# Moving the output banks and three early chunks into the projections' PSUM banks, with a fifth first-layer weight buffer

## The chip, the cores and the metric

The kernel runs on one NeuronCore of a Trainium2 chip, as one program. The metric is the device time of one execution in microseconds (us), as the median of several runs. The engines are TensorE (PE, with its weight loads as PEld), VectorE (DVE), ScalarE (ACT), GpSimd (POOL) and SyncE (SP), which here only issues DMAs. They run side by side, each through its own instructions in a fixed order, and wait for each other by semaphores.

## What is computed

Three layers in a row, all in fp32: random-feature attention, a network with `h - tanh(h)` between two matrices, and a mixture of four networks with `relu`, weighted by token. Cut to what matters:

```python
def phi(x):                                  # x: (2, 8, 576, 64), omega: (128, 64)
    proj = einsum('bhsd,md->bhsm', x, omega)
    h = proj - sum(x * x) / 2
    return exp(h - max(h)) / sqrt(128)
q_p, k_p = phi(q * scale), phi(k * scale)
num = q_p @ (k_p.T @ v)                      # per batch and head
x = num / (q_p @ sum(k_p) + 1e-6)            # -> (1152, 512)
h = x @ w_in                                 # 512 -> 2048, first network
x = (h - tanh(h)) @ w_out                    # 2048 -> 512
p = probs / sum(probs)
out = sum_e p[:, e] * (relu(x @ w1[e]) @ w2[e])   # 4 networks, 512 -> 1024 -> 512
```

## The kernel before

**Matrices in two parts.** Every operand of a large product is split (`split`, L70) into a high part (ACT) and the rest (DVE, or POOL where `nc.gpsimd` is given), and each product is three matmuls: high·high, high·low, low·high. The weights of the first network arrive as 64-bit numbers and are put together by `Decoded` (L94): ACT `scaled` and `topped` or DVE `joined`, then `parted`, in which ACT makes the high part (`wah`, `wbh`) and POOL the low one (`wal`, `wbl`). They lie in the pool `wp` with `NJ` = 4 buffers of each name. `load_a(i, j)` is tile j (128 hidden units) of unit i (512 hidden units) of `w_in`; `ready` (L163) does all steps of a tile at once.

**Attention.** Tokens are taken in groups; the queries in 12 units (4 pairs of heads × 3 chunks of tokens, L389), and the loop at L485 works on four units at once, each a step further: transpose (`psT`) and project (`psP`, two banks of `ps_p`), turn the features (`psQ`), multiply (`psN`), transpose back (`psX`) and split into `xT`, the four pairs of tiles `x0p`, `x1p` of the first network's input (in rows `x`).

**Early chunks.** The first network's first unit (i = 0) does not wait for all tokens. `early(e)` (L471) takes tile j = e mod 4 and token chunk n = e div 4, with 512, 384 and 256 columns for n = 0, 1, 2: twelve matmuls (`hidden`, L426, rows at L435) into one bank, `pse`, of the pool `ps_e` (2 banks), then `minus_tanh` (L441) on it: ACT `u`, `t`, `q` and `m`, DVE `a`, `b`, `s` and `c`, ACT `h` and POOL `l`. In rows they are u L445, y L446, t L447, u L448 on ACT, y L449, y L450, pse L451, y L452 on DVE, hh L453 on ACT and hl L454 on POOL. L452, the copy-predicated, is the last to read the bank. e0 to e7 are started in the loop at L485, e8 to e11 behind it (L498), and after e8, e9 and e10 one tile of unit 1 (`load_a` (1,0), (1,1), (1,2)) is made ready; it takes the weight buffers of the tile that this chunk read last.

**First network.** After `actx.close()` (L502) the eight PSUM banks are given out anew: `ps_o` (2 banks, output chunks `po`), `ps_hb` and `ps_ha` (3 each, `psh`, the hidden tiles of unit 1 and later). `ps_o` comes first and lies where `ps_e` lay. `out_a` (L526) makes one output chunk of 384 columns in twelve matmuls (rows at L539); the loop at L705 puts out chunks and hidden tiles in turn. The first output chunk reads columns 0 to 383 of unit 0, the third columns 768 to 1151. A pool that opens with `reuse_waits="tile"` makes each new tile wait for the last users of just the banks or bytes it covers.

**Second network.** From about 290 us on; it reads `w1` through `wa` tiles of `wp` as well, on every other step from a pool of its own (`high`, L601).

**Order.** Up to the loop at L705 a scheduler sets the order on each engine, from the program's order and the tiles; it may move a step ahead of others. From L701 on, and again from L799, the order on DVE, PE and ACT is written out by hand. DMAs stand in program order on SP's queue.

Of the kernel before, what the change touches and what calls it, by code (L numbers as in the profile page):

```python
# [8 lines left out]
F32 = mybir.dt.float32  # L9
F32R = mybir.dt.float32r  # L10
# [16 lines left out]
def tile_favor_attention__then__two_moe(  # L27
# [19 lines left out]
    B, H, S, D = q.shape  # L47
# [4 lines left out]
    P = 128  # L52
    NP = H // 2
# [3 lines left out]
    UF = 512  # L57
    NJ = UF // P
# [7 lines left out]
    wp = ctx.enter_context(tc.tile_pool(name="wp", bufs=NJ))  # L66
# [3 lines left out]
    def split(hi, lo, src, eng_lo=None):  # L70
        nc.scalar.activation(hi, src, AF.Copy)  # L71
        (eng_lo or nc.vector).tensor_tensor(out=lo, in0=src, in1=hi.bitcast(F32), op=ALU.subtract)  # L72

    def run(todo):
        for step in todo:
            step()
# [14 lines left out]
    PLAIN = 2  # L91
    wa, wb, late = {}, {}, {}

    class Decoded:  # L94


# [26 lines left out]
            nc.vector.scalar_tensor_tensor(out=m, in0=self.up, scalar=SIGN, in1=m, op0=ALU.bitwise_and, op1=ALU.bitwise_or)  # L123

        def parted(self):
            hi = wp.tile([P, UF], F32R, tag=self.tag + "h", name=self.tag + "h")
            lo = wp.tile([P, UF], F32R, tag=self.tag + "l", name=self.tag + "l")
            split(hi, lo, self.m.bitcast(F32), nc.gpsimd)
            return hi, lo

    class Loaded:
# [10 lines left out]
        joined = scaled  # L142

        def parted(self):
            hi = self.pool.tile([P, UF], F32R, tag=self.tag + "h", name=self.tag + "h")
            lo = self.pool.tile([P, UF], F32R, tag=self.tag + "l", name=self.tag + "l")
            split(hi, lo, self.raw)
            return hi, lo

# [13 lines left out]
    def ready(load, table, *ij):  # L163
        w = load(*ij)
        w.scaled()
        w.joined()
        table[ij] = w.parted()
# [11 lines left out]
    actx = ExitStack()  # L179
    ps_e = actx.enter_context(tc.tile_pool(name="ps_e", bufs=2, space=bass.MemoryType.PSUM))  # L180
    ac = actx.enter_context(tc.tile_pool(name="ac", bufs=1))
    a2 = actx.enter_context(tc.tile_pool(name="a2", bufs=2))
    a3 = actx.enter_context(tc.tile_pool(name="a3", bufs=3))
    ps_t = actx.enter_context(tc.tile_pool(name="ps_t", bufs=2, space=bass.MemoryType.PSUM))
    ps_p = actx.enter_context(tc.tile_pool(name="ps_p", bufs=2, space=bass.MemoryType.PSUM))
    ps_n = actx.enter_context(tc.tile_pool(name="ps_n", bufs=2, space=bass.MemoryType.PSUM))
    kctx = ExitStack()
    kp = kctx.enter_context(tc.tile_pool(name="kp", bufs=2, side="right"))
    TD = TB * D
# [10 lines left out]

        nc.sync.dma_start(out=to, in_=x[b, :, REST, :].rearrange("h r d -> r h d"))

    om = ac.tile([P, 2, D], F32, name="om")
    nc.sync.dma_start(out=om, in_=omega.rearrange("m (o d) -> m o d", o=1).to_broadcast([M, 2, D]))

    def load_k(p):
# [40 lines left out]

    pso = ps_t.tile([P, 512], F32, tag="t", name="pso")
    nc.tensor.transpose(pso[:, :P], om.rearrange("p j d -> p (j d)"), ident)
    oms = ac.tile([P, P], F32, name="oms")  # L250
    nc.scalar.mul(oms, pso[:, :P], scale)
    ob = [ac.tile([P, 2 * P], F32R, name=f"ob{a}") for a in range(2)]
    for a in range(2):
# [138 lines left out]
    def q_emit(u, what, i):  # L392
        if 0 <= u < len(q_units):
            if u not in q_steps:
                p, n = q_units[u]
                qf = a3.tile([P, TB, 2, M], F32, tag="xf", name="qf")
                rest = qr[:, 2 * p:2 * p + 2, :].rearrange("p h d -> p (h d)")
                T, R = features(lambda b, h: qn[:, b, 2 * p + h], rest, chunks[n], qf, a2)
                A, Z, X = q_products(p, chunks[n], qf)
                q_steps[u] = dict(T=T, R=R, A=A, Z=Z, X=X)  # L400
            if i < len(q_steps[u][what]):
                q_steps[u][what][i]()
# [19 lines left out]
    def new_g(i, j):  # L422
        pool = late["hpb"] if i % 2 or i >= NA else hpa
        gs[i, j] = tuple(pool.tile([P, N], F32R, tag="h" + z, name="h" + z) for z in "hl")

    def hidden(i, j, chunks=range(NC), bank=None, kks=range(KD)):  # L426
        if bank is None and chunks[0] == 0 and kks[0] == 0:
            ph[i, j] = late["ps_hb" if j % 2 else "ps_ha"].tile([P, NC, 512], F32, tag="h", name="psh")
        wh, wl = wa[i, j]
        for kk in kks:  # L430
            c = slice(kk * P, (kk + 1) * P)
            xh, xl = state["x"][kk]
            for z, (w, x) in enumerate(((wh, xh), (wh, xl), (wl, xh))):
                for n in chunks:
                    nc.tensor.matmul(  # L435
                        ph[i, j][:, n, :CH] if bank is None else bank, w[:, c],
                        x[:, n * CH:(n + 1) * CH] if bank is None else x[:, n],
                        start=z == 0 and kk == 0, stop=z == 2 and kk == KD - 1,
                    )
# [31 lines left out]
    def early(e):  # L471

        j, n = e % NJ, e // NJ
        if n == 0:
            new_g(0, j)
        s = slice(chunks[n][0][0] * P, (chunks[n][-1][0] + chunks[n][-1][1]) * P)
        w = s.stop - s.start
        ps = ps_e.tile([P, 512], F32, tag="e", name="pse")[:, :w]
        hidden(0, j, [s], ps)
        t, u, y = (a2.tile([P, 512], F32, tag=z, name=z)[:, :w] for z in "tuy")  # L480
        g = minus_tanh(ps, gs[0, j][0][:, s], gs[0, j][1][:, s], t, u, y, lambda z: z, nc.gpsimd)
        run(g[x] for x in "utqambsch" + "l")

    NU = len(q_units)
    for u in range(1, NU + 3):  # L485
        q_emit(u, "R", 0)
        q_emit(u - 1, "A", 0)
        q_emit(u - 2, "Z", 0)
        q_emit(u + 1, "T", 0)
        q_emit(u, "R", 1)  # L490
        q_emit(u - 1, "A", 1)
        q_emit(u - 2, "Z", 1)
        q_emit(u - 3, "X", 0)
        if u >= NP + 3:
            early(u - NP - 3)
        if u in LATER:
            ready(*LATER[u])
    for e in range(NU - NP, NU):  # L498
        early(e)
        if e < NU - 1:  # L500
            ready(load_a, wa, 1, e % NJ)
    actx.close()  # L502


# [13 lines left out]
    late["gp"] = moe1.enter_context(tc.tile_pool(name="gp", bufs=1, side="right", reuse_waits="tile"))  # L518
    late["hpb"] = ctx.enter_context(tc.tile_pool(name="hpb", bufs=NJ, reuse_waits="tile"))
    accp = ctx.enter_context(tc.tile_pool(name="accp", bufs=1, reuse_waits="tile"))  # L520
    ps_o = ctx.enter_context(tc.tile_pool(name="ps_o", bufs=2, space=bass.MemoryType.PSUM, reuse_waits="tile"))
    plain = ExitStack()
    for z in ("ps_hb", "ps_ha"):
        late[z] = plain.enter_context(tc.tile_pool(name=z, bufs=1, space=bass.MemoryType.PSUM, reuse_waits="tile"))
# [47 lines left out]
    class Sums:  # L572
# [28 lines left out]
        def high(self, i):  # L601
            src, names = self._dest(i)
            pool = wp if self.q % 2 else late["wp"]
            w = [pool.tile([P, UF], F32R, tag="wa" + z, name="wa" + z) for z in "hl"]
            w = [x.rearrange("p (s k n) -> p s k n", s=2, n=P) for x in w]
            for s, name in enumerate(names):
                self.lhs[name] = (w[0][:, s], w[1][:, s])
            if i == 0:
                w = [x.rearrange("p s k n -> p (s k) n") for x in w]
            elif i == 3:  # L610
                w = [x[:, 0] for x in w]
            self.w = src, w[0], w[1]
            nc.scalar.activation(w[0], src, AF.Copy)
# [295 lines left out]
```

## Time and profile before

| | us |
|---|---|
| median of 3 runs | 692.48 (691.49 to 692.78) |
| profiled execution, its own time | 694.46 |
| its span | 692.6 |
| PE busy in the span | 671.7 (97%) |
| DVE busy | 530.7 (77%) |
| ACT busy | 318.0 (46%) |
| POOL busy | 61.3 (9%) |

Times in the profile count from the start of the span. PE is the engine that is nearly always busy, so the time is its work and its few gaps. A row of a timeline gives start, duration, engine, line, operation, output<-input by the program's names, shape and count; in square brackets stand the engine's idle time just before and the instruction that ended it. Matmuls overlap: a row's duration is longer than the step from one start to the next.

### The profile page before, as it was taken

Reading aid. Unit: us, or ns where it says so; the run is one execution under the profiler, and the core shown is the slowest. Engines: PE = TensorE matmul, PEld = TensorE weight load, DVE = VectorE, ACT = ScalarE, POOL = GpSimd, SP = SyncE. Lnnn points to the kernel's source line nnn. Section 1 sums busy time; section 2 is a strip of 40 time slices with the busy share of each in tenths; the row PEclk is TensorE's granted clock in tenths of the full one; section 3 lists DMA queues with packets and bytes.
Section 4 is the critical chain, followed back from the end, with each engine's and each line's share of the span. In section 5 each row is a group of like instructions: output and inputs, shape, how many; then the busy total and the mean of one; then the engine's idle time right before and its main releaser. Section 6 shows DMA issues by size and latency. Waiting matters only on the chain.

```text
span 692.6 us, 10155 instructions
## 1 busy us (share of the span) xinstructions
PE 671.7 (97%) x4059; PEld 624.7 (90%) x4059; DVE 530.7 (77%) x824; ACT 318.0 (46%) x591; POOL 61.3 (9%) x58
## 2 busy tenths in 40 slices
PE   6999998899999999899999999999999999999997
PEld 5899987899999999799999899999998999999996
DVE  4599888589999987769467687777777777777664
ACT  5699898576775754435123222322222322223120
POOL 1032023412321210000000000000000000000000
PEclk9999999999999999999999999999999999999999
DMA  8953110022221222101110112111210211120004
GB/s 223 280 164 115 62 32 1 31 76 79 92 91 62 92 62 91 31 1 62 30 31 31 55 38 62 31 40 53 61 31 31 62 49 44 31 62 1 1 0 137
DMA packets 42766, 43.72 MB, mean 63 GB/s; under 512 B 5600, under 2 KB 37600, under 8 KB 42720
## 3 DMA queue, kind: packets, MB, share of 16 engines
q1 hardware_dynamic: 42720, 43.08, 20.5%
q8 instruction: 32, 0.52, 0.3%
q14 instruction: 14, 0.11, 0.1%
HBM read 40.72 MB, written 2.36 MB: 62 GB/s over the span
## 4 chain that ended last, share of the span: by engine, by line
PE 75%; DVE 13%; ACT 6%; issue 2%; DMA 1%; SPq 1%; POOL 0%; DVEq 0%; POOLq 0%
PE po L660 28%; PE Y L643 22%; PE psh L435 7%; PE po L539 6%; PE pse L435 3%; PE psP L294 2%; PE psN L346 2%; DVE y L449 2%; DVE y L452 2%; DVE y L450 1%; ACT y L446 1%; DVE psh L451 1%; ACT u L445 1%; DVE m L123 1%; DVE m L122 1%
## 5 line engine op out<-in xcount | busy, mean ns | idle before, releaser
L666 DVE SCALAR_TENSOR_TENSOR oacc<-po,pr,oacc 128x512 f32<-128x512 f32 (+1 forms) x136 | 101.4, 746 | 34.2 <-PE po L660 33.8
L660 PE MATMUL po<-wbh,hl 128*128 128x512 f32 x290 | 112.9, 389 | 0.4 <-DVE hl L466 0.4
L660 PE MATMUL po<-wbh,hh 128*128 128x512 f32 x290 | 112.9, 389 | 0.1
L660 PE MATMUL po<-wbl,hh 128*128 128x512 f32 x290 | 112.9, 389 | 0.0
L660 PEld LDWEIGHTS po<-wbh,hl 128*128 128x128 f32 x290 | 54.4, 188 | 12.3 <-DVE hl L466 0.8
L539 PE MATMUL po<-hh,wbh 128*128 128x384 f32 x180 | 61.4, 341 | 2.1 <-DVE y L452 1.8
L660 PEld LDWEIGHTS po<-wbh,hh 128*128 128x128 f32 x290 | 54.7, 188 | 8.2 <-DVE oacc L666 0.3
L539 PE MATMUL po<-hh,wbl 128*128 128x384 f32 x180 | 61.1, 339 | 0.5 <-POOL wbl L72 0.5
L539 PE MATMUL po<-hl,wbh 128*128 128x384 f32 x180 | 61.3, 340 | 0.2 <-DVE hl L454 0.2
L660 PEld LDWEIGHTS po<-wbl,hh 128*128 128x128 f32 x290 | 54.4, 188 | 7.5
L821 ACT ACTIVATE hh<-Y 128x576 fp32r<-128x576 f32 x42 | 27.4, 653 | 72.5 <-DVE Y L818 64.0
L435 PE MATMUL psh<-x,wah 128*128 128x384 f32 x288 | 58.4, 338 | 0.6 <-ACT wah L71 0.6
L643 PE MATMUL Y<-y,wah 128*128 128x288 f32 x336 | 57.9, 294 | 0.0
L643 PEld LDWEIGHTS Y<-y,wah 128*128 128x128 f32 x336 | 51.2, 188 | 3.6 <-DVE hl L466 0.3
L435 PEld LDWEIGHTS psh<-x,wah 128*128 128x128 f32 x288 | 51.1, 190 | 0.8 <-ACT wah L71 0.8
L643 PE MATMUL Y<-Th,wal 128*128 128x288 f32 x224 | 47.8, 295 | 0.0
L643 PE MATMUL Y<-Tl,wah 128*128 128x288 f32 x224 | 47.6, 294 | 0.0
L643 PE MATMUL Y<-Th,wah 128*128 128x288 f32 x224 | 47.6, 293 | 0.0
L821 ACT ACTIVATE hh<-u 128x576 fp32r<-128x576 f32 x14 | 9.6, 688 | 73.5 <-DVE u L818 73.5
L643 PEld LDWEIGHTS Y<-Th,wah 128*128 128x128 f32 x224 | 39.0, 188 | 4.5
L453 ACT ACTIVATE hh<-y 128x1152 fp32r<-128x1152 f32 (+3 forms) x24 | 20.4, 848 | 43.1 <-DVE y L452 43.1
L539 PEld LDWEIGHTS po<-hh,wbh 128*128 128x128 f32 x180 | 34.2, 190 | 2.9 <-DVE y L452 2.0
(138 smaller groups left out, 1459.3 us busy)
## 6 DMA issues: line engine op xcount, KB each, us to landing
raw<-in_moe_w_dram SPq DMA_DIRECT2D x30, 512.0 KB, 3.5
raw<-in_moe_w_in_dram SPq DMA_DIRECT2D x16, 512.0 KB, 3.6
raw<-in_moe_w_out_dram SPq DMA_DIRECT2D x16, 512.0 KB, 3.4
kn<-in_k_dram SPq DMA_DIRECT2D x8, 256.0 KB, 4.7
vs<-in_v_dram SPq DMA_DIRECT2D x8, 256.0 KB, 4.6
qn<-in_q_dram SPq DMA_DIRECT2D x8, 256.0 KB, 4.8
out_dram<-oacc SPq DMA_DIRECT2D x7, 256.0 KB, 2.3
raw<-in_moe_w_dram SPq DMA_DIRECT2D x4, 256.0 KB, 3.6
```

The lines of the kernel that those rows point to most:

```text
L122: nc.vector.scalar_tensor_tensor(out=m, in0=self.y.bitcast(I32), scalar=3, in1=m, op0=ALU.logical_shift_left, op1=ALU.bitwise_or)
L294: nc.tensor.matmul(ps[:, i].rearrange("p a m -> p (a m)"), x[:, c], o, start=j == 0, stop=j == 2)
L346: nc.tensor.matmul(ps[:, j, h, :ZC], qt[g][:, j, h, :], kvz[p][:, t // (TB + 1), h, :], start=True, stop=True)
L435: nc.tensor.matmul(ph[i, j][:, n, :CH] if bank is None else bank, w[:, c], x[:, n * CH:(n + 1) * CH] if bank is None else x[:, n], start=z ...
L449: a=lambda: vec.scalar_tensor_tensor(out=y, in0=y, scalar=CB, in1=u, op0=ALU.add, op1=ALU.mult),
L452: c=lambda: vec.copy_predicated(view(y), view(u).bitcast(I32), ps),
L453: h=lambda: act.activation(hh, y, AF.Copy),
L539: nc.tensor.matmul(po[:, :CH], w[:, r], g[:, s], start=j == 0 and z == 0, stop=j == NJ - 1 and z == 2,)
L643: nc.tensor.matmul(ps[:, m, :HN // 2], w[:, kk], b[:, m * HN // 2:(m + 1) * HN // 2], start=first and kk == 0 and z == 0, stop=kk == 1 and ...
L660: nc.tensor.matmul(po, g[:, s], w[:, cols], start=j == 0 and z == 0, stop=j == 1 and z == 2)
L666: nc.vector.scalar_tensor_tensor(out=acc, in0=po, scalar=pr[:, t, e:e + 1], in1=acc, op0=ALU.mult, op1=ALU.add)
L821: nc.scalar.activation(halves(gs[NA + q, f][0][:, h * HN:(h + 1) * HN]), x, AF.Relu)
```

## The change

Four edits. The pools `ps_n` and `ps_p` swap places, and `ps_o` opens from the right side, so that it lies where `ps_p` lay; `ps_hb` and `ps_ha` then lie where `ps_e`, `ps_t` and `ps_n` lay. The early chunks 5, 7 and 9 go to banks of `ps_p` (NP = 4). First-layer weights get a fifth buffer in `wp`, and tiles (1,0), (1,1), (1,2) are made ready one place earlier. To make room, `om` and `oms` go from the pool `ac` to `kp`.

```diff
+    def halves_of(pool, tag):
+        bufs = NJ + (pool is wp and tag == "wa")
+        return [pool.tile([P, UF], F32R, tag=tag + z, name=tag + z, bufs=bufs) for z in "hl"]
...
-            hi = wp.tile([P, UF], F32R, tag=self.tag + "h", name=self.tag + "h")
-            lo = wp.tile([P, UF], F32R, tag=self.tag + "l", name=self.tag + "l")
+            hi, lo = halves_of(wp, self.tag)
...
+    ps_n = actx.enter_context(tc.tile_pool(name="ps_n", bufs=2, space=bass.MemoryType.PSUM))
     ps_p = actx.enter_context(tc.tile_pool(name="ps_p", bufs=2, space=bass.MemoryType.PSUM))
-    ps_n = actx.enter_context(tc.tile_pool(name="ps_n", bufs=2, space=bass.MemoryType.PSUM))
...
-    om = ac.tile([P, 2, D], F32, name="om")
+    om = kp.tile([P, 2, D], F32, name="om", bufs=1)
...
-    oms = ac.tile([P, P], F32, name="oms")
+    oms = kp.tile([P, P], F32, name="oms", bufs=1)
...
-        ps = ps_e.tile([P, 512], F32, tag="e", name="pse")[:, :w]
+        pool, tag = (ps_p, "p") if e in (NP + 1, NP + 3, 2 * NP + 1) else (ps_e, "e")
+        ps = pool.tile([P, 512], F32, tag=tag, name="pse")[:, :w]
...
+        if u == NU + 1:
+            ready(load_a, wa, 1, 0)
     for e in range(NU - NP, NU):
         early(e)
-        if e < NU - 1:
-            ready(load_a, wa, 1, e % NJ)
+        if e < NU - 2:
+            ready(load_a, wa, 1, e % NJ + 1)
...
-    ps_o = ctx.enter_context(tc.tile_pool(name="ps_o", bufs=2, space=bass.MemoryType.PSUM, reuse_waits="tile"))
+    ps_o = ctx.enter_context(tc.tile_pool(name="ps_o", bufs=2, space=bass.MemoryType.PSUM, side="right", reuse_waits="tile"))
```

`halves_of` also serves `Loaded.parted` and `high`. The scheduler then sets another order in the passage. Three places, before and now (numbers behind names tell tiles apart):

On PE, behind the early chunk e8 (`pse_1655` before), the first hidden tile of unit 1 (`psh_1841`) is put between chunks; before:

```order
L435 MATMUL pse_1655<-x03_665,wal_358 128x256
L435 MATMUL psh_1841<-x00_659,wah_1689 128x384 x3
L435 MATMUL psh_1841<-x10_660,wah_1689 128x384 x3
L435 MATMUL psh_1841<-x00_659,wal_1690 128x384 x3
L435 MATMUL psh_1841<-x01_661,wah_1689 128x384
L435 MATMUL pse_1693<-x00_659,wah_476 128x256
```

and now, where it stands behind e10 (`pse_1743`) and ahead of e11 (`pse_1769`):

```order
L437 MATMUL pse_1743<-x03_665,wal_731 128x256
L437 MATMUL psh_1841<-x00_659,wah_1632 128x384 x3
L437 MATMUL psh_1841<-x10_660,wah_1632 128x384 x3
L437 MATMUL psh_1841<-x00_659,wal_1633 128x384 x3
L437 MATMUL psh_1841<-x01_661,wah_1632 128x384 x3
L437 MATMUL psh_1841<-x11_662,wah_1632 128x384 x3
L437 MATMUL psh_1841<-x01_661,wal_1633 128x384
L437 MATMUL pse_1769<-x00_659,wah_811 128x256
```

Ten matmuls of it stood between e8 and e9 and eight between e9 and e10; now sixteen stand between e10 and e11, and two behind e11, ahead of the first output chunk.

On PE, around the back-transposes of the last attention unit (`psX`, the source of the last columns of `x03`, `x13`), before, where they stand ahead of e7 (`pse_1629`):

```order
L435 MATMUL pse_1598<-x03_665,wah_730 128x384
L435 MATMUL pse_1598<-x13_666,wah_730 128x384
L435 MATMUL pse_1598<-x03_665,wal_731 128x384
L361 MATMUL psX_1624<-ident_67,xs_1437 128x128 x2
L435 MATMUL pse_1629<-x00_659,wah_811 128x384
```

and now, where they stand inside e8 (`pse_1667`), and e9 (`pse_1705`) and e10 (`pse_1743`) are put between the parts of e8; the transposes, and later the first matmul of e8 on `x13`:

```order
L437 MATMUL pse_1667<-x01_661,wah_357 128x256
L363 MATMUL psX_1636<-ident_67,xs_1437 128x128 x2
L437 MATMUL pse_1667<-x11_662,wah_357 128x256
L437 MATMUL pse_1667<-x01_661,wal_358 128x256
L437 MATMUL pse_1667<-x02_663,wah_357 128x256
```

```order
L437 MATMUL pse_1705<-x03_665,wah_476 128x256
L437 MATMUL pse_1743<-x00_659,wah_730 128x256
L437 MATMUL pse_1743<-x10_660,wah_730 128x256
L437 MATMUL pse_1743<-x00_659,wal_731 128x256
L437 MATMUL pse_1743<-x01_661,wah_730 128x256
L437 MATMUL pse_1667<-x13_666,wah_357 128x256
L437 MATMUL pse_1667<-x03_665,wal_358 128x256
```

Twenty matmuls of 256 columns stand between the transposes and that one. On DVE `x13` stands behind the four steps of e6.

On POOL, the low part of unit 1's first tile stood behind the second-round `hl` of e4 to e6; before:

```order
L72 TENSOR_TENSOR wbl_1141<-m_1136,wbh_1140 128x512
L454 TENSOR_TENSOR hl_1211<-y_1227,hh_1210 128x512
L454 TENSOR_TENSOR hl_1297<-y_1313,hh_1296 128x512
L454 TENSOR_TENSOR hl_1378<-y_1394,hh_1377 128x512
L454 TENSOR_TENSOR hl_1450<-y_1466,hh_1449 128x512
L454 TENSOR_TENSOR hl_1211<-y_1526,hh_1210 128x384
L454 TENSOR_TENSOR hl_1297<-y_1573,hh_1296 128x384
L454 TENSOR_TENSOR hl_1378<-y_1613,hh_1377 128x384
L72 TENSOR_TENSOR wal_1690<-m_1685,wah_1689 128x512
```

and now stands ahead of the first `hl`, that of e0:

```order
L72 TENSOR_TENSOR wbl_1141<-m_1136,wbh_1140 128x512
L72 TENSOR_TENSOR wal_1633<-m_1628,wah_1632 128x512
L456 TENSOR_TENSOR hl_1211<-y_1227,hh_1210 128x512
L456 TENSOR_TENSOR hl_1297<-y_1313,hh_1296 128x512
L456 TENSOR_TENSOR hl_1378<-y_1394,hh_1377 128x512
```

Its high part moved on ACT likewise. DVE's two joins and ACT's `m` for tile (1,3) moved from e8's steps to those of e4 and e3.

## Rows read from the trace of the kernel before

**Rows 1.** Busy time by stretch: start:end, length, each engine, TensorE's granted clock, DMA.

```profile
core 0: us, PE busy (x) PEld busy (x) DVE busy (x) ACT busy (x) POOL busy (x), PEclk, DMA share, GB/s
84.00:100.00 16.00, 16.00 (x106) 13.89 (x107) 13.51 (x36) 14.22 (x35) 2.57 (x2) 1.00 0.12 34
112.00:118.00 6.00, 4.03 (x24) 3.50 (x24) 4.04 (x9) 4.76 (x12) 1.91 (x2) 1.00 0.00 0
118.00:129.30 11.30, 8.21 (x55) 7.41 (x55) 9.11 (x18) 9.15 (x24) 8.00 (x8) 1.00 0.15 48
129.30:135.00 5.70, 5.70 (x24) 5.70 (x25) 2.20 (x5) 3.53 (x8) 1.60 (x3) 0.70 0.01 1
...
290.00:310.00 20.00, 19.26 (x98) 18.55 (x99) 10.58 (x20) 5.18 (x10) 0.00 (x0) 0.91 0.00 1
```

**Rows 2.** PE's timeline, 113 to 130: e7, e8, first hidden tile, e9, e11, first output.

```profile
113.37 0.61 PE L435 MATMUL pse<-x,wah 128*128 128x384 f32 x2 [1.46 <-DVE y L452]
...
115.87 0.51 PE L435 MATMUL pse<-x,wah 128*128 128x256 f32 x2 [0.16 <-DVE y L452]
...
117.27 0.28 PE L435 MATMUL pse<-x,wal 128*128 128x256 f32 x1
118.15 1.31 PE L435 MATMUL psh<-x,wah 128*128 128x384 f32 x6 [0.60 <-ACT wah L71]
119.74 0.79 PE L435 MATMUL psh<-x,wal 128*128 128x384 f32 x3 [0.28 <-POOL wal L72]
...
121.84 0.28 PE L435 MATMUL pse<-x,wal 128*128 128x256 f32 x1
...
125.79 0.51 PE L435 MATMUL pse<-x,wah 128*128 128x256 f32 x2 [0.85 <-DVE y L452]
...
129.28 0.44 PE L539 MATMUL po<-hh,wbh 128*128 128x384 f32 x1 [1.81 <-DVE y L452]
```

**Rows 3.** DVE's timeline: L449 of e5 and e6, `x13`, L452 of e8 and e9.

```profile
110.38 0.98 DVE L449 SCALAR_TENSOR_TENSOR y<-y,u 128x384 f32<-128x384 f32 x1
...
113.30 0.56 DVE L449 SCALAR_TENSOR_TENSOR y<-y,u 128x384 f32<-128x384 f32 x1
113.77 0.42 DVE L72 TENSOR_TENSOR x<-psX,x 128x256 fp32r<-128x256 f32 x1
...
122.76 0.44 DVE L452 COPY_PREDICATED y<-u,pse 128x256 f32<-128x256 int32 x1
...
125.29 0.44 DVE L452 COPY_PREDICATED y<-u,pse 128x256 f32<-128x256 int32 x1
```

**Rows 4.** POOL's timeline: the low parts `hl` of e0, e4 and e11.

```profile
89.62 1.28 POOL L454 TENSOR_TENSOR hl<-y,hh 128x512 fp32r<-128x512 f32 x1 [20.94 <-ACT hh L453]
...
109.92 1.03 POOL L454 TENSOR_TENSOR hl<-y,hh 128x384 fp32r<-128x384 f32 x1 [1.27 <-ACT hh L453]
...
132.35 0.74 POOL L454 TENSOR_TENSOR hl<-y,hh 128x256 fp32r<-128x256 f32 x1 [1.65 <-ACT hh L453]
```

**Rows 5.** ACT's timeline: high part of tile (1,0), `m` of tile (1,3).

```profile
117.47 0.63 ACT L71 ACTIVATE wah<-m 128x512 fp32r<-128x512 f32 x1
...
120.02 0.67 ACT L113 ACTIVATE m<-raw 128x512 int32<-128x512 uint32 x1
```

**Rows 6.** ACT's waits from 100 to 136: us in total, times, longest.

```profile
ACT u L448 <- DVE y L449: 1.7, 3, 0.8
ACT u L445 <- PE pse L435: 1.7, 2, 1.2
ACT wah L71 <- PE pse L435: 1.1, 2, 0.5
```

**Rows 7.** Chain that ended last, 128 to 140: the first three output chunks.

```profile
129.28 3.52 PE po L539 x12
...
134.77 2.08 PE po L539 x12
...
138.41 1.73 PE po L539 x10
```

More of the change, by code (lines that the diff above doesn't have):

```diff
@@ L144, in parted @@
         def parted(self):
-            hi = self.pool.tile([P, UF], F32R, tag=self.tag + "h", name=self.tag + "h")
-            lo = self.pool.tile([P, UF], F32R, tag=self.tag + "l", name=self.tag + "l")
+            hi, lo = halves_of(self.pool, self.tag)
             split(hi, lo, self.raw)
@@ L603, in high @@
             pool = wp if self.q % 2 else late["wp"]
-            w = [pool.tile([P, UF], F32R, tag="wa" + z, name="wa" + z) for z in "hl"]
+            w = halves_of(pool, "wa")
             w = [x.rearrange("p (s k n) -> p s k n", s=2, n=P) for x in w]
```

## The prediction

> **What bounds the kernel now.** I read the stretches first, then TensorE's timeline in the one stretch where it idles, then the queues it waits for. In [rows 1] PE is busy all 16.00 us of 84 to 100, but only 4.03 of 6.00 us from 112 to 118 and 8.21 of 11.30 us from 118 to 129.3; behind that it is busy without a gap. This is the passage from attention into the first network: the last early chunks (e8 to e11 and the end of the wider ones) and the first output chunk. So 1.97 + 3.09 = 5.06 us of PE idle lie in 17 us, and little before them.
>
> [Rows 2] name each gap and what ended it. Four are banks: e7 (1.46 us at 113.37), e8 (0.16), e11 (0.85) and the first output chunk `po` (1.81 at 129.28) each wait for the copy-predicated (L452) that frees the bank two tiles back. Two are the weights of unit 1's first tile: `wah` (0.60, ACT) and `wal` (0.28, POOL). Together 5.16 us. A listed gap begins at the modelled end of the matmul ahead, and a matmul of 256 columns stands as 0.28 us in a row [rows 2], while twelve of 384 take 2.08 us on the chain [rows 7], 0.173 each, or 0.12 for 256; so each gap holds about 0.16 us more in which a next matmul could have started: 5.16 + 6 × 0.16 = 6.1 us.
>
> Then comes a second price. From 129.3 to 135 PE is busy throughout, yet its granted clock is 0.70 [rows 1], a mixture of the two levels (1.2 and 2.4 GHz): (1 − 0.70) × 2 × 5.70 = 3.4 us at the lower, where half of the work is lost, 1.7 us. What PE did before it fell: it idled 0.85 and 1.81 us within the last 4.4 us. The 1.46 us at 113.37 were followed by no fall (1.00 from 112 to 118). From there on PE sets the pace, so what is won ahead of 135 stays won.
>
> **The change part by part.** *Banks of the early chunks.* e5, e7 and e9 go into the projections' pair, idle since unit 11's projection; e6, e8, e10, e11 keep the other pair. A bank is now reused three or four chunks later, not two: e6 takes e3's bank, e8 e4's, e10 e6's, e11 e8's, e9 e5's; e5 and e7 take projections' banks. How long a chunk holds its bank: e8's last matmul starts at 117.27 [rows 2] and its L452 ends at 122.76 + 0.44 = 123.20 [rows 3], 5.9 us; e9's runs from 121.84 to 125.73, 3.9 us. For e7 and e8 at least 2.1 us more PE work (one chunk of 12 × 0.173) stands in between, and the waits of 1.46 and 0.16 are gone. For e11 the new order leaves, behind e8's last matmul, 10 matmuls of 256 columns and 16 of 384: 10 × 0.12 + 16 × 0.173 = 4.0 us of cover for 3.9 to 5.9 us. What remains is 0 to 1.9; I take 0.2, since e8's 5.9 hold ACT work for the next weights (below), which is off the way now, and e9's is the nearer row.
>
> *Output banks.* `po` takes the projections' pair, so its first chunk waits for e9, not e10, and its second for e7. Behind e9's last matmul stand 8 matmuls of e10, 16 of unit 1, 12 of e11, 2 of unit 1: 20 × 0.12 + 18 × 0.173 = 5.5 us against 3.9 to 5.9. Remains 0 to 0.4; I take 0.1. Unit 1's second tile gets the banks of e10 and e11, but it stands three output chunks later.
>
> *Fifth weight buffer.* Tile (1,0) needs no bank of e8's weights back, so its split runs before the first early chunk: POOL has 20.94 us idle there [rows 4], ACT's 0.63 us `wah` of (1,0) and 0.67 us `m` of (1,3) [rows 5] leave the tight stretch, and the two gaps of 0.60 and 0.28 go. Where they land, ACT is busy 14.22 of 16.00 us and PE all of it [rows 1]: between nothing and the full 1.3 us may show there. I take 0.1, as ACT still has 1.8 us free. DVE's two joins for (1,3) go ahead too, among e4's steps; PE is still a chunk ahead there, so they are bounded with it. The DMAs stand in the same order on SP's queue. `om` and `oms` only change pool, no instruction; cost nothing.
>
> *What is late next: ACT, POOL and the last chunk.* PE may come 5.7 us early, but ACT has only 1.7 + 1.7 + 1.1 = 4.5 us of waits to give [rows 6], and 1.1 us of moved work (0.63 and 0.67 overlap their neighbours by 0.1 each). So the last `hl`, which POOL ends at 132.35 + 0.74 = 133.09 [rows 4], comes between 133.1 and 127.5. Its first reader is the tenth matmul of the third output chunk, 138.41 + 9 × 0.173 = 140.0 now [rows 7], 132.6 then. Price 0 to 0.5 us; I take 0, for half a microsecond out of those 5.6 is enough.
>
> *Clock.* With gaps of 0.3 us left there is nothing like the 0.85 and 1.81 us, so I take all 1.7 us back. The later lower stretch (0.91 over 20 us from 290 to 310, some 3.5 us at the lower level [rows 1]) follows waits at the end of the first network that the change does not touch; I leave it, with up to 1.7 us either way in the bounds.
>
> **Sum:** gaps 6.1 − 0.2 − 0.1 − 0.1 = 5.7, clock 1.7: 7.4 us. The profiled span goes from 692.6 to 685.2 and that execution from 694.46 to 687.1. It stands 1.98 us above the median of the runs; from the median, 692.48 − 7.4 = **685.1 us**. With every bound at its worst (1.9 + 0.4 + 1.3 + 0.5 remaining, no clock) 2.0 us are gained, with all at its best 6.1 + 1.7 + 1.7 = 9.5.
>
> **Rule against row.** DVE's L449 at 110.38 takes 0.98 us, the same form 0.56 at 113.30; the long one begins inside POOL's `hl` (109.92 to 110.95) [rows 3, 4]. The Trainium skill, "SBUF — State Buffer", section "Who interferes with whom", says that a VectorE instruction with two SBUF inputs and a GpSimd instruction that reads SBUF exclude each other, whoever issues first. The row agrees with it. It speaks against the change, because it packs POOL's pieces closer; by the rows, that is the second rival.
>
> **Rivals.** *A: the clock gives nothing in the timed runs*, because it does not fall there now, or falls again. For it: the same kernel's runs differ by 1.29 us, and a gap of 1.46 us cost no clock. Then 5.7 us: 686.8. The Trainium skill, "TensorE: Matmul & The Clock Gate", section "What's actually happening", says that the activity is judged on a schedule that does not start with the kernel; by that rule, too, one execution can lose what another keeps. No single trace can show it.
>
> *B: DVE and POOL in each other's way.* From e6 on six L449 remain. If each loses 0.42 us (0.98 − 0.56) and the bank waits return by as much, 2.5 us of the 7.4 go, and with a gap at `po` long enough the clock may go as well: 687.6 to 689.3. Against: DVE has 2.0 and 2.2 us free in the two stretches [rows 1], and bank reuse is no longer two tiles back.
>
> *C: slower.* The order now puts the rest of e8, e9 and e10 behind one matmul that reads `x13` of the last unit. Before, PE transposed that unit ahead of e7, and `x13` was there at 113.77 + 0.42 = 114.19 [rows 3]. Now the transposes stand after e7 and four matmuls of e8, and `x13` stands on DVE behind e6's whole chain. PE would reach it some 2.4 us (20 × 0.12) after the transposes; ACT and DVE need 0.4 + 0.4 us plus their queues. Each us that `x13` is later than that stops PE for one, with nothing left to fill it. It turns into a loss when it is over 7.4 + 1.4 us late, at 694 or more. Against: the chain ahead of it is four instructions of about 0.5 us.
>
> *D: nothing happens*, because some other reader holds the same banks: 692.5. Against: `po`'s only DVE wait is then e9's, which PE has left 5.5 us before.
>
> **How the numbers follow.** My forecast (685.1, with the later clock stretch falling as before or not) 0.66, A 0.17, B 0.10, C 0.03, D 0.04. The range of 683.4 to 687.6 holds the forecast with 1.7 us of clock to the good, A, and the near end of B; the rest, far B, C and D, is under 2 in 10. About 0.2% (1.4 us) is what a measurement of this kernel can tell from no change. Faster: forecast, A and B, 0.93; same: D, 0.04; slower: C, 0.03.
>
> **What would show it.** Right: in the new profile PE's gaps between 100 and 130 are below about 0.5 us in sum, the first output chunk starts near 129.28 − 5.7 = 123.6, its twelve matmuls take 2.1 us and not the 3.5 of [rows 7], and the granted clock stays at 1.00 there; everything behind is shifted by the same 7.4 us. Wrong: a wait of e10 or e11 on L452 above 1 us, PE waiting for `x13` or for ACT's `x`, a lower clock after `po`, or a gap newly found before 100. A gain under 5 us would mean that ACT's or DVE's chain and not the banks set the pace.

## The result

| | before | after |
|---|---|---|
| median (lowest to highest, runs) | 692.57 us (691.49 to 692.78, 4) | 685.12 us (683.68 to 686.84, 4) |
| profiled execution, its span | 692.6 us | 684.4 us |
| PE busy in the span | 671.7 us (97%) | 668.2 us (98%) |

The ratio of after to before is 0.99, 95% interval 0.9873 to 0.9928: faster by 7.45 us in the medians, where 7.4 was forecast. Two later groups of runs gave 0.9892 (0.9874 to 0.991) and 0.9899 (0.9878 to 0.992). All timed runs of the study together, 64 of before and 15 of after, have medians of 691.9 and 684.8: 7.1 us.

The same five stretches as in [rows 1], of the kernel after:

```profile
84.00:100.00 16.00, 16.00 (x115) 13.72 (x114) 13.20 (x33) 14.40 (x36) 2.57 (x2) 1.00 0.11 34
112.00:118.00 6.00, 6.00 (x46) 6.00 (x45) 5.25 (x14) 5.09 (x13) 2.70 (x3) 1.00 0.02 6
118.00:129.30 11.30, 11.27 (x71) 10.74 (x71) 7.61 (x19) 10.20 (x27) 7.19 (x8) 1.00 0.00 1
129.30:135.00 5.70, 5.70 (x35) 5.70 (x34) 3.75 (x6) 4.84 (x7) 0.98 (x2) 1.00 0.18 58
290.00:310.00 20.00, 20.00 (x117) 20.00 (x116) 13.46 (x23) 7.16 (x12) 0.00 (x0) 1.00 0.13 43
```

PE is busy 6.00 of 6.00 and 11.27 of 11.30 us where it was busy 4.03 and 8.21. From 112 to 118 it has 46 matmuls instead of 24. The granted clock is 1.00 in both stretches that showed 0.70 and 0.91. What this passage looks like from PE and along the chain of work that ended last (the edit moves lines: L435, L449, L452 and L539 are now L437, L451, L454 and L544, and a little further on in some experiments):

```profile
114.98 0.38 PE L363 MATMUL psX<-ident,xs 128*128 128x128 f32 x2
...
118.99 1.21 PE L437 MATMUL psh<-x,wah 128*128 128x384 f32 x6
120.04 0.68 PE L437 MATMUL psh<-x,wal 128*128 128x384 f32 x3
120.56 1.20 PE L437 MATMUL psh<-x,wah 128*128 128x384 f32 x6
121.60 0.34 PE L437 MATMUL psh<-x,wal 128*128 128x384 f32 x1
121.83 0.51 PE L437 MATMUL pse<-x,wah 128*128 128x256 f32 x2
...
123.35 0.51 PE L437 MATMUL psh<-x,wal 128*128 128x384 f32 x2
123.89 0.44 PE L544 MATMUL po<-hh,wbh 128*128 128x384 f32 x1
124.17 0.34 PE L544 MATMUL po<-hl,wbh 128*128 128x384 f32 x1
124.35 0.34 PE L544 MATMUL po<-hh,wbl 128*128 128x384 f32 x1
```

```profile
115.36 3.79 PE pse L437 x32
119.15 2.79 PE psh L437 x16
121.94 1.57 PE pse L437 x12
123.51 0.35 PE psh L437 x2
123.86 0.03 issue
123.89 2.35 PE po L544 x12
```

No row bears an idle time in brackets any more. The chain is PE from end to end, and the first twelve `po` take 2.35 us where [rows 7] had 3.52. The two waits that matter most, at e11 and at `po`, are hidden but for 0.06 and 0.19 us. DVE's copy-predicated (L452 before, L454 now) of e8 and of e9:

```profile
121.33 0.44 DVE L454 COPY_PREDICATED y<-u,pse 128x256 f32<-128x256 int32 x1
...
123.38 0.45 DVE L454 COPY_PREDICATED y<-u,pse 128x256 f32<-128x256 int32 x1
```

e8's ends at 121.77, and e11, which takes its bank, starts at 121.83. PE was done with the matmul ahead at 121.60 + 0.17 = 121.77: cover and wait are equal. e9's ends at 123.83, PE was done at 123.35 + 2 × 0.17 = 123.70, and `po` starts at 123.89: 0.19 us are left of the 1.81.

**Where the 8.2 us of the two profiles come from.** I set the starts of the same matmuls side by side. At 75 us after is 1.0 us late; its matmuls keep the longer step of the lower clock until about 13.6 us, those of before until about 10.6. The other two profiles of after are 0.8 and 0.55 us early there, so the late start belongs to this execution and not to the change. At the first `po` it is 5.39 early (129.28 − 123.89): the passage gave 6.4. At 143 us it is 6.97 early: the twelve `po` at full clock gave 1.58. That holds to 285 us but for 0.06 (6.91). At 300 us it is 8.17 early, since the clock did not fall there, which gave 1.26, and so it stays to the end. 1.0 − 6.4 − 1.6 + 0.1 − 1.3 = −8.2.

### The profile page after: what moved, and what is told of

The parts are those of the page before. It is cut to its first block, busy times and chain, and to the rows that moved or that the text cites. A ratio compares the mean times of both kernels' runs of the same rounds, so it can differ in the third digit from the quotient of the medians.

```text
span 684.4 us, 10149 instructions
## 1 busy us (share of the span) xinstructions
PE 668.2 (98%) x4059; PEld 622.5 (91%) x4059; DVE 528.5 (77%) x824; ACT 317.2 (46%) x591; POOL 61.3 (9%) x58
## 4 chain that ended last, share of the span: by engine, by line
PE 77%; DVE 13%; ACT 5%; issue 2%; DMA 2%; SPq 1%; DVEq 0%
PE po L665 29%; PE Y L648 23%; PE psh L437 7%; PE po L544 6%; PE pse L437 4%; PE psP L296 3%; PE psN L348 2%; DVE y L454 2%; DVE y L451 1%; DVE y L452 1%; DVE psh L453 1%; ACT y L448 1%; DVE m L127 1%; DVE m L126 1%; ACT m L117 1%
## 5 line engine op out<-in xcount | busy, mean ns | idle before, releaser
L544 PE MATMUL po<-hh,wbh 128*128 128x384 f32 x180 | 60.8, 338 | 0.3
L544 PE MATMUL po<-hh,wbl 128*128 128x384 f32 x180 | 60.5, 336 | 0.5 <-POOL wbl L72 0.5
L544 PE MATMUL po<-hl,wbh 128*128 128x384 f32 x180 | 60.7, 337 | 0.3 <-DVE hl L456 0.2
L437 PE MATMUL psh<-x,wah 128*128 128x384 f32 x288 | 57.7, 336 | 0.0
L437 PEld LDWEIGHTS psh<-x,wah 128*128 128x128 f32 x288 | 50.5, 188 | 0.0
L618 ACT ACTIVATE wah<-y 128x512 fp32r<-128x512 f32 x28 | 17.6, 631 | 41.1 <-DVE y L598 41.1
```

The lines of the kernel that those rows point to most:

```text
L437: nc.tensor.matmul(ph[i, j][:, n, :CH] if bank is None else bank, w[:, c], x[:, n * CH:(n + 1) * CH] if bank is None else x[:, n], start=z ...
L544: nc.tensor.matmul(po[:, :CH], w[:, r], g[:, s], start=j == 0 and z == 0, stop=j == NJ - 1 and z == 2,)
```

## Experiments

Each timed kernel stands beside runs of before on its own chip. "Passage" is what PE has gained on before between 102 us and the first `po` (waits alone), or up to the second round of output chunks at 143 us where the text says so. It is read from the starts of the same matmuls, so that a late start of the program doesn't count. Not run were the two moves of banks without the fifth buffer, and the swap of the pools by itself.

| kernel | ratio to before (95%) | median, us | passage, us |
|---|---|---|---|
| after | 0.9892 (0.9874 to 0.991) | 684.3 | 6.42 |
| without the fifth buffer | 0.9931 (0.9915 to 0.9947) | 686.99 | 4.88 |
| output banks without the chunks' | 0.9944 (0.9931 to 0.9957) | 687.94 | 3.95 |
| fifth buffer alone | 0.9972 (0.996 to 0.9984) | 689.99 | 1.96 |
| chunks' banks and buffer, output banks as before | 0.998 (0.9968 to 0.9992) | 689.93 | 1.62 |
| before, with matmuls put into its last wait | 0.9997 (0.9986 to 1.0009) | 691.36 | 0.01 |

### The kernel after, again

No edit.

> The changed kernel once more, to see how far its own executions differ and whether the clock falls in them. Theory 1 (waits and clock): the part from 84 to 135 us is the same as in its first profile, no gap of PE above 0.3 us and no lower clock there, in every execution; what differs between executions, 683.7 to 686.8 so far, comes from other places: the start (the first profile was 1.0 us later by 13 us than the profile of before) and the end of the first network (a lower clock or none). Theory 2 (chance of the clock): the executions at 686 and more are those in which the clock falls in the passage again; their mean granted clock would be about 0.9975 for one such fall of 3.4 us.

Measured: 684.3 (683.23 to 685.89, 5 runs) against 691.7. In its profile the passage gave 6.42 again, and the clock stayed at 1.00: theory 1 holds for this execution. Theory 2 is half true. Of the 15 runs of after, nine have a mean granted clock of 0.999 or 1.000 and a median of 684.0, six have 0.996 to 0.998 and 685.7; so the clock does fall in the longer ones. The only profile of after with a fall has it at 283 us (below), not in the passage.

### Without the fifth buffer

```diff
-        bufs = NJ + (pool is wp and tag == "wa")
+        bufs = NJ
...
-        if u == NU + 1:
-            ready(load_a, wa, 1, 0)
...
-        if e < NU - 2:
-            ready(load_a, wa, 1, e % NJ + 1)
+        if e < NU - 1:
+            ready(load_a, wa, 1, e % NJ)
```

> The changed kernel without the fifth buffer of first-layer weights: four buffers, and tiles (1,0), (1,1), (1,2) made ready behind e8, e9, e10 as before. Banks as in the change. Theory 1 (each wait belongs to its own resource and the parts add up): the two gaps for wah and wal return, 0.60 + 0.28 and 0.16 for each, 1.2 us: 686.3. Theory 2 (one chain): with banks free PE only comes to the next wait earlier, so the missing buffer shows as a larger gap further down, at e11 or at the first output chunk, of 1.5 to 2 us, and with the lower clock behind it: 687 to 689.

Measured: 686.99, 2.7 us above after, at the near end of theory 2; the lower clock that it expected is not in the profile. PE's timeline shows where the passage loses 1.54 (6.42 − 4.88):

```profile
120.93 0.50 PE L437 MATMUL pse<-x,wah 128*128 128x256 f32 x2 [1.31 <-DVE y L454]
...
124.37 0.45 PE L542 MATMUL po<-hh,wbh 128*128 128x384 f32 x1 [0.25 <-DVE y L454]
```

These are bank waits of e11 and `po`, not the weight waits of 0.60 and 0.28 that the buffer was to remove. What delays the release stands in POOL's and ACT's timelines:

```profile
116.25 1.30 POOL L72 TENSOR_TENSOR wal<-m,wah 128x512 fp32r<-128x512 f32 x1 [1.36 <-ACT wah L71]
117.50 1.02 POOL L456 TENSOR_TENSOR hl<-y,hh 128x384 fp32r<-128x384 f32 x1
...
118.56 0.51 ACT L448 ACTIVATE y<-u,ca 128x256 f32<-128x256 f32 x1 [0.98 <-POOL hl L456]
```

The weights' low part stands on POOL ahead of a chunk's `hl`, ACT's `y` needs the buffer that this `hl` reads, and the bank's release is behind `y`. The release is the copy-predicated on DVE, and e11 starts right behind it. ACT's waits from 108 to 128 list it so, here and in after:

```profile
ACT y L448 <- POOL hl L456: 3.0, 3, 1.1
```

```profile
ACT y L448 <- POOL hl L456: 1.1, 2, 0.9
```

With the buffer, the first weight tile is split before the first chunk, and `hl` comes ahead of `wal` there. So its worth is mostly that it takes weight steps out of the way of the banks' release.

### The fifth buffer alone

```diff
-        pool, tag = (ps_p, "p") if e in (NP + 1, NP + 3, 2 * NP + 1) else (ps_e, "e")
+        pool, tag = (ps_e, "e")
...
-    ps_o = ctx.enter_context(tc.tile_pool(name="ps_o", bufs=2, space=bass.MemoryType.PSUM, side="right", reuse_waits="tile"))
+    ps_o = ctx.enter_context(tc.tile_pool(name="ps_o", bufs=2, space=bass.MemoryType.PSUM, reuse_waits="tile"))
```

The pools `ps_n` and `ps_p` stay swapped.

> The kernel before with the fifth buffer of first-layer weights and its earlier tiles alone; all early chunks in their own pair of banks and the output banks there too, as before. Theory 1 (the parts add up): the gaps for wah and wal go, 1.2 us: 691.4. Theory 2 (one chain): the bank waits of e11 and of the first output chunk take over what is won, since their banks come free no earlier: less than 0.7 us, 691.9 to 692.6, with the clock falling as before.

Measured: 689.99, and 1.96 us in the passage, more than either theory gave it. The waits that stay:

```profile
112.26 0.62 PE L437 MATMUL pse<-x,wah 128*128 128x384 f32 x2 [0.36 <-DVE y L454]
...
124.97 0.50 PE L437 MATMUL pse<-x,wah 128*128 128x256 f32 x2 [1.91 <-DVE y L454]
127.07 0.45 PE L544 MATMUL po<-hh,wbh 128*128 128x384 f32 x1 [0.42 <-DVE y L454]
```

e7's wait fell from 1.46 [rows 2] to 0.36 and `po`'s from 1.81 to 0.42, though no bank was added. e11's grew from 0.85 to 1.91: with two banks it still waits for e9's copy-predicated, and PE now reaches it earlier. So the buffer alone moves the waits to e11.

### Output banks as before

```diff
-    ps_o = ctx.enter_context(tc.tile_pool(name="ps_o", bufs=2, space=bass.MemoryType.PSUM, side="right", reuse_waits="tile"))
+    ps_o = ctx.enter_context(tc.tile_pool(name="ps_o", bufs=2, space=bass.MemoryType.PSUM, reuse_waits="tile"))
```

The chunks' banks and the fifth buffer stay.

> The changed kernel with the output banks where they were (in the early chunks' own pair, so the first output chunk waits for e10); early chunks 5, 7, 9 in the projections' banks and the fifth buffer stay. Theory 1 (the parts add up): the gap ahead of the first output chunk stays, 1.81 + 0.16 us, and the 1.6 us of lower clock behind it, so 3.6 us of 7.4 are lost: 688.7. Theory 2 (one chain): the chunks' own gain only moves the stop, PE waits as much longer for e10's copy-predicated as it comes earlier: 691 to 692.6.

Measured: 689.93; 1.62 us in the passage, against 6.42 with this one word.

```profile
122.01 0.79 PE L437 MATMUL pse<-x,wah 128*128 128x256 f32 x2 [2.68 <-DVE y L454]
...
128.87 0.44 PE L544 MATMUL po<-hh,wbh 128*128 128x384 f32 x1 [0.63 <-DVE y L454]
```

Neither theory had the right chunk. `po` waits (0.63), but for e11 and not for e10: with three chunks gone to other banks, e11 is the ninth in the pair of `ps_e` and lies in its first bank, the one that the first `po` takes. The last of the four copy-predicateds of 256 columns on DVE is e11's; here and in after it is

```profile
128.37 0.45 DVE L454 COPY_PREDICATED y<-u,pse 128x256 f32<-128x256 int32 x1
```

```profile
128.25 0.46 DVE L454 COPY_PREDICATED y<-u,pse 128x256 f32<-128x256 int32 x1
```

Here it ends at 128.82, and `po` starts at 128.87. In after it ends at 128.71, 4.82 us behind the start of `po` (123.89), and 4.8 us is all that the passage loses (6.42 − 1.62). The 2.68 us ahead of e11 are a part of that and no second price. With `ps_o` on the left, `ps_ha` lies where the projections' banks were, which now hold e5, e7 and e9, and the scheduler puts all eighteen matmuls of unit 1's first tile behind e11, sixteen of which covered its wait; they stand ahead of `po` instead. A lower clock follows the 2.68 us (0.51 from 121.7 to 125.2): the row says 0.79 for two matmuls where 0.51 is usual. Up to `po` it costs nothing, for the chain that ended last doesn't run through PE there:

```profile
122.83 1.28 POOL wal L72
124.11 0.70 POOL hl L456
...
124.83 0.52 ACT y L448
...
128.37 0.46 DVE y L454
```

### Output banks without the chunks'

```diff
-        pool, tag = (ps_p, "p") if e in (NP + 1, NP + 3, 2 * NP + 1) else (ps_e, "e")
+        pool, tag = (ps_e, "e")
```

> The changed kernel with all early chunks in their own pair of banks (reused two chunks later, as before); the output banks in the projections' pair and the fifth buffer stay. Theory 1 (the parts add up): the gaps at e7, e8 and e11 stay, 1.46 + 0.16 + 0.85 and 3 x 0.16, 2.95 us, the clock does not fall as the longest gap is 1.5 us: 685.1 + 2.95 = 688.1. Theory 2 (one chain): PE reaches e11 earlier and waits longer there, 2 us and more, the clock falls behind it: 689.5 to 691.

Measured: 687.94, 3.6 us above after's 684.3, though `ps_o` is free long before it is needed. Two waits are listed in the passage:

```profile
111.69 0.62 PE L437 MATMUL pse<-x,wah 128*128 128x384 f32 x2 [0.37 <-DVE y L454]
...
114.77 0.97 PE L437 MATMUL psh<-x,wah 128*128 128x384 f32 x4 [0.49 <-DVE x L72]
```

The first output matmul stands early (121.17), and chunks that wait for banks stand behind it; the second round of output chunks is 5.53 us earlier than before's, 1.58 of it clock, so 3.95 of waits. The time is that of theory 1 (688.1), the waits are not: e7's came back as 0.37 instead of 1.46, e11's is not listed at all, and one for `x` is new. By the steps from start to start the two listed waits cost 1.4 of the 2.5 us that are lost against after; the rest lies mostly in delays of some 0.3 us each, without a listed idle time, at 108.6, 119.1, 124.5 and 131.8 us.

The parts don't add up: taken away from the whole they cost 1.5 (buffer), 2.5 (chunks' banks) and 4.8 us (output banks), 8.8 together for a gain of 6.4, and the buffer alone gives 2.0. Each covers a wait that the others shift.

### Matmuls in the last wait of before

```diff
+    fill = ps_t.tile([P, 512], F32, tag="t", name="fill")
+    h = gs[0, 1][0]
+    for i in range(12):
+        nc.tensor.matmul(fill[:, :256], h[:, N - 256:N - P], h[:, N - 256:], start=True, stop=True)
```

This is the kernel before with twelve matmuls that nobody reads, put between e11 and the first output chunk. They shorten no chain; they only keep PE at work while it runs.

> The kernel before, with twelve extra matmuls of 256 columns (1.4 us of PE work, into a free bank, read by nobody) behind the last early chunk, in the place where PE idled 1.81 us ahead of the first output chunk. All waits stay. Theory 1 (the idle lowers the clock): the first output chunk still starts near 129.3 us, its twelve matmuls take 2.1 us in place of 3.5, the granted clock from 129.3 to 135 is 1.00, and the time falls by about 1.6 us to 691.0. Theory 2 (the lower clock has another cause, and the gain of the change is waits alone): the fall stays, the time is 692.6 or, with the extra work in the way, up to 1.4 us more.

Measured:

```profile
128.46 0.44 PE L543 MATMUL po<-hh,wbh 128*128 128x384 f32 x1 [0.39 <-DVE y L452]
```

The first `po` starts when it did (129.28, less 0.82 by which this execution is early from its first 40 us on), PE idles 0.39 there instead of 1.81, and the granted clock stays at 1.00: the twelve `po` were 1.58 us shorter in the trace. But the median moved by 0.3 us, no difference (0.9986 to 1.0009), where theory 1 had 1.6.

The granted clock that stands beside every timed run tells why. One fall of 3.4 us at half the clock takes 0.0025 off the mean of a run. Of the 60 runs of before beside the experiments, 18 have a mean of 0.996 or less (median 692.6 us), 24 have 0.997 or 0.998 (691.8) and 18 have 0.999 or 1.000 (690.8). Averaged, the clock lost is 1.6 us a run in before, 1.3 with the fillers (12 runs) and 0.9 in after (15 runs). So the fillers took 0.3 us of it away and the change 0.8. Where in a run the clock fell these means don't say; three more profiles of before were to tell.

### The kernel before, three more profiles

No edit.

> The kernel before, unchanged, profiled once more to see in how many executions TensorE's granted clock falls behind the first output chunk (at about 130 us) and behind the end of the first network (about 290 us). First theory (the waits cause the falls every time): both again, a stretch of 0.70 between 129.3 and 135 and of 0.91 between 290 and 310, twelve matmuls of the first output chunk in about 3.5 us, span about 692. Rival A (the fall happens in some executions only): in this and the next two profiles the fall at 130 us is missing in at least two of the three, twelve matmuls in about 2.1 us, and the span is then 1.3 to 1.7 us shorter for each missing fall, 689 to 691. The run with the filler matmuls, whose timed median moved by 0.3 us where its trace showed 1.58 us, speaks for the rival: by it about one execution in five has the fall.

> A second further profile of the kernel before, with the same expectations: first theory, the falls at 130 and 290 us stand again (0.70 and 0.91 by stretch); rival A, the one at 130 us stands in about one profile of five, so most likely not here, and the span is 689 to 691.

> A third further profile of the kernel before, with the same expectations: first theory, the falls at 130 and 290 us stand again; rival A, the one at 130 us most likely doesn't. Together with the first profile and the two others, four in all: four falls at 130 us would be the first theory, one or two the rival.

Measured: spans of 688.8, 688.5 and 692.4 us. The clock fell at 130 us in one of the three, so in two of four with the first profile; the same two have the fall at 290. The rival holds, though its "one in five" was too low. What sets the two kinds apart stands in DVE's and POOL's timelines, at e10's L449 and the low part `hl` of e9. Third profile, with the fall:

```profile
126.73 0.73 POOL L454 TENSOR_TENSOR hl<-y,hh 128x256 fp32r<-128x256 f32 x1
126.74 1.01 DVE L449 SCALAR_TENSOR_TENSOR y<-y,u 128x256 f32<-128x256 f32 x1 [1.15 <-ACT y L446]
```

First of the three, without:

```profile
126.30 0.42 DVE L449 SCALAR_TENSOR_TENSOR y<-y,u 128x256 f32<-128x256 f32 x1 [1.15 <-ACT y L446]
126.31 1.01 POOL L454 TENSOR_TENSOR hl<-y,hh 128x256 fp32r<-128x256 f32 x1
...
128.32 0.45 PE L539 MATMUL po<-hh,wbh 128*128 128x384 f32 x1 [1.48 <-DVE y L452]
```

The two start 0.01 us apart here (0.02 and 0.05 in the other two profiles), and whichever starts second takes 1.0 us instead of 0.42 (DVE) or 0.73 (POOL). Where POOL is first, e10's copy-predicated is late and `po` waits 1.81 and 1.83 us; where DVE is first, 1.48 in both. A lower clock followed the longer wait both times and the shorter neither time. The profile with the fillers belongs to the first kind:

```profile
126.04 0.74 POOL L454 TENSOR_TENSOR hl<-y,hh 128x256 fp32r<-128x256 f32 x1
126.06 1.00 DVE L449 SCALAR_TENSOR_TENSOR y<-y,u 128x256 f32<-128x256 f32 x1 [1.15 <-ACT y L446]
```

There PE worked through most of the wait, and the clock didn't fall. Five executions can't tell whether the longer wait is what made the clock fall or only came with it.

### The last hidden tile in thirds

```diff
-        run(g[x] for x in "schl")
+        run(g[x] for x in "sc")
+        (hh, hl), y = gs[NA - 1, NJ - 1], last_y[-1]
+        for n in range(NC):
+            s = slice(n * CH, (n + 1) * CH)
+            nc.scalar.activation(hh[:, s], y[:, s], AF.Copy)
+            nc.vector.tensor_tensor(out=hl[:, s], in0=y[:, s], in1=hh[:, s].bitcast(F32), op=ALU.subtract)
```

A version beyond the change, at the longest waits that it leaves: the end of the first network, where the last chunks wait for the whole of `hh` and `hl` and read a third.

> The kernel after, with one thing more: of the first network's last hidden tile the steps h (ACT copy) and l (DVE subtraction) are done in three column thirds, each copy followed by its subtraction, so that an output chunk of 384 columns waits for its own third only. It aims at the two longest waits of TensorE that the change left, 1.20 us for hh and 0.95 us for hl at 282 to 284 us, 2.1 us together. First theory (these waits are the length of two full-width steps of 1152 columns): they fall to 0.6 us in sum, the time to 1.5 us under the kernel after's 684.3, so 682.8. Rival (another wait stands right behind, an x or a weight tile, or the smaller steps cost ACT and DVE as much): the waits stay above 1.5 us in sum and the time is 684.3 within 0.5 us.

> The kernel after once more, on the same chip as the one with the steps in thirds, to compare these two directly, and a third profile of it for the clock. Expected 684.3 again (683.8 to 685.1), the first output chunk within 0.2 us of 130 less 6.4 less the start's shift, and no lower clock between 120 and 310: first theory, that after the change the passage no longer holds a wait that a lower clock follows. Rival: the clock falls in some executions of after too, at 283 to 300 behind the waits of 1.20 and 0.95 us.

> The kernel with the last hidden tile's h and l in column thirds, beside the kernel after on one chip. First theory: its trace showed TensorE's way from the last matmul before the wait for hh to the first high by low one behind it shorter by 1.45 us, and the timed median is that much under the kernel after's: 1.2 to 1.6 us. Rival: the waits come back further on in the timed runs, and the two medians stand within 0.5 us of each other.

Measured: 683.74 and 683.88 (682.29 to 684.27), after on the second chip 685.08 (683.92 to 685.89). PE's timeline there, of after:

```profile
280.86 0.45 PE L544 MATMUL psh<-hh,wbh 128*128 128x384 f32 x1 [1.18 <-ACT hh L455]
282.25 0.44 PE L544 MATMUL psh<-hl,wbh 128*128 128x384 f32 x1 [0.95 <-DVE hl L456]
```

and of the kernel with thirds:

```profile
280.64 0.45 PE L546 MATMUL psh<-hh,wbh 128*128 128x384 f32 x1 [0.54 <-ACT hh L751]
```

The wait for `hl` is gone and the one for `hh` halved; against after the matmuls behind are 1.46 us earlier in both traces. So the first theory's waits came out (0.54 in sum). In the medians it is 1.2 us on one chip. The two kernels' intervals against before overlap (0.9856 to 0.9898 and 0.9878 to 0.992), and the runs of after there have a lower mean clock (0.998 against 0.999), so part of the 1.2 is clock: the gain is shown by the traces and only likely by the times. Of after's three profiles this last one has a lower clock by those two waits (0.83 from 280 to 290), the two others don't: the rival named with it is true for that place. Behind the first output chunk none of the three has one.

## Why the prediction was right

**Gaps, 5.7 forecast.** The passage gave 6.42 in all three profiles of after, against the first profile of before, and 6.0 against those two whose `po` waited 1.48 us. The forecast was low for two reasons. Of the rests of 0.2 (e11) and 0.1 (`po`), 0.06 and 0.19 were found, and nothing of the 0.1 for work moved ahead of 100 us: PE is busy 16.00 of 16.00 there with ACT at 14.40. And the second matmul after a wait starts later than the pitch: 0.28 us behind the first at `po` (123.89 to 124.17), where 0.17 is the pitch (124.17 to 124.35). Four waits ahead of the first `po` are gone with this (e7, e8, `wah`, `wal`), 4 × 0.1 us more than the 6.1 counted; e11 and `po` have it still.

The estimate of a chunk's hold of its bank, 3.9 rather than 5.9 us, was the right end: in after e8's last matmul starts ten short ones ahead of 118.99, at 117.7, and its copy-predicated ends at 121.77, 4.1 us, just covered by 4.0 us of matmuls. The reason given was right in part. A `wah` of 0.63 us, that of the next tile, stands on ACT ahead of e8's first step in after too (117.89). What left are ACT's `m` and, not counted in the forecast, two joins that stood between e8's steps on DVE in before:

```profile
120.72 0.69 DVE L122 SCALAR_TENSOR_TENSOR m<-y,m 128x512 int32<-128x512 int32 x1
...
122.00 0.85 DVE L123 SCALAR_TENSOR_TENSOR m<-raw,m 128x512 int32<-128x512 int32 x1
```

**Clock, 1.7 forecast.** In the trace the size held: 1.58 us. That PE's idling makes the clock fall is not shown. As a term of the timed sum it was too large. The fall stood in two of four profiles of before, so about half of it, 0.8 us, belongs in the median, and 0.8 us is what the mean clocks of the timed runs give. What I took from one execution as a property of the kernel was an event of some executions. 6.0 to 6.4 from the waits and 0.8 from the clock make the 7.1 us of all runs. The runs of either kernel with a mean clock of 0.999 or 1.000 stand 6.7 us apart (690.8 and 684.0), a little above the waits alone. That the 7.4 of the forecast met the first 7.45 so closely is in part luck: one term was 0.5 too small, the other 0.9 too large, and the first four runs stood 0.35 above all runs.

**Rival A** (no clock in the timed runs, 686.8) was half true in its reason and wrong in its time: the waits alone gave more than the 5.7 it kept. **Rival B** (DVE and POOL) described something real, but in the kernel before: there it makes `po`'s wait 1.48 or 1.83. In after the exclusion strikes where it costs nothing:

```profile
108.38 1.78 POOL L456 TENSOR_TENSOR hl<-y,hh 128x512 fp32r<-128x512 f32 x1 [5.17 <-ACT hh L455]
...
128.79 1.56 POOL L456 TENSOR_TENSOR hl<-y,hh 128x256 fp32r<-128x256 f32 x2
```

The first takes 1.78 us where [rows 4] had 1.28; the last two take 1.56 together, where one took 0.74 [rows 4], and DVE's L451 (L449 before) keeps its 0.55 and 0.42. The Trainium skill, "SBUF — State Buffer", section "Who interferes with whom", says that the two exclude each other and that the order of issue decides who waits. The rows agree with it; the pairs of 126.73 and 126.30 show it turned both ways by 0.01 us. **Rival C**: `x13` came at 116.61 + 0.41 = 117.02, some 1.7 us behind its transposes (114.98 + 0.38), where 2.4 us of matmuls covered it; PE waited for it nowhere. **Rival D**: each wait named went or fell under 0.2 us.

**ACT and the last `hl`.** Priced at 0. It ends at 128.79 + 1.56 = 130.35, and its first reader stands in the third output chunk, which starts at 131.28. That is the eleventh matmul, not the tenth of the forecast (the tenth reads `hh`, by the order of `po`'s rows), at 131.28 + 10 × 0.17 = 133.0: 2.6 us to spare.

**Not foreseen:** the clock at 290 us. I had left it as before, with 1.7 us either way; the profile gained 1.3 there, but before shows the fall in two of four profiles and after in one of three, with the same waits of 1.2 and 0.95 us ahead of it in all seven; so it can't be credited to the change.

## What to carry to other kernels

When a stage's buffers close and the next stage's open, ask on which bank the first new tile falls: the one released last is the worst, and choosing the side that was idle moved more here (4.8 of 6.4 us) than the extra buffers. Moving some users out of a pair of banks can change which one is the last in the bank that the next stage takes: with the output banks on the left it was e11 instead of e10. Judge such a change whole: the weight buffer alone moved a wait to the next reader (0.85 to 1.91 us at e11), and in the whole it paid mostly because it took weight steps out of the way of a bank's release, not for its own wait. Before an event like a clock fall is put into a sum, profile the kernel several times, read the mean clock of the timed runs, and take the share of executions that show it.

## What the runs showed of the hardware

Two instructions that start 0.01 to 0.05 us apart on DVE and POOL decide by their order which of them takes 1.0 us, and by that 0.35 us of PE's wait, in one and the same program. A stretch at the lower granted clock (1.2 of 2.4 GHz) cost 0.7 us (after, third profile, where part of it lay in the waits themselves), 1.3 (before, at 290) or 1.58 us (before, at 130). The wait ahead of it doesn't settle whether one follows: 1.81, 1.83 and 2.68 us were followed by one and 1.91 us (fifth buffer alone, at e11) was not. Waits of 1.2 and 0.95 us at the end of the first network stand in before's four profiles and after's three; one followed in two and in one of them. It also followed with the fifth buffer alone and with the output banks as before (0.91 and 0.88 from 290 to 300 us), and not in the other three kernels that have these waits.
